# A SwiGLU behind attention: the last head pair's late loads in a new order, and PSUM banks as a ring of pairs

## The chip, the cores and the metric

The kernel runs on one core of a Trainium2 chip. The metric is device time in microseconds (us). A core has five engines that run their own instruction streams: TensorE (PE, matrix products into PSUM), VectorE (DVE), ScalarE (ACT), GpSimd (POOL) and SyncE (SP, which mostly issues DMAs; ACT issues some too). They wait for each other through semaphores.

## The reference, cut to what matters

```
def _attn_ref(q, k, v):                       # 4 x 8 x 576 x 64
    q_rot, k_rot = (rotate(q), rotate(k))
    scores = scale * np.matmul(q_rot, k_rot.transpose(0, 1, 3, 2))
    scores = scores - np.max(scores, axis=-1, keepdims=True)
    attn = np.exp(scores)
    attn = attn / (np.sum(attn, axis=-1, keepdims=True) + 1e-09)
    return np.matmul(attn, v).astype(np.float32)

def _moe_ref(x, w_gate, w_val, w_out):        # x: 2304 x 512, d_ff 1536
    g = x @ w_gate
    silu = g * (1.0 / (1.0 + np.exp(-g)))
    val = x @ w_val
    return (silu * val @ w_out).astype(np.float32)
```

x is the attention's result with the heads side by side: 4 batches of 576 rows make 2304 tokens. The inputs are float32, except that the weights enter the kernel as 64-bit words, of which DVE, ACT and POOL make a high and a low float32 part. Every product is made of three matmuls (high by high, high by low, low by high).

## The kernel before, in words

**Attention.** 32 heads make 16 pairs p of 9 blocks b of 128 rows; n counts the 144 blocks. For each block PE makes the scores (sc), DVE their row maxima (L364), ACT the exponential (L382), PE transposes it (tr, L425) and later multiplies by V (pv, L465). ACT copies the results (Y, L470), which go to device memory (yd: L484, L489, L490). Row sums go there as their reciprocals (rd, L403) and come back spread over partitions (R, rload, L630). During the last pairs, POOL already makes the tokens' high and low parts for the SwiGLU: `xload` (L637) brings Xab, `xprep` (L644 to L647) adds, multiplies by R and splits into xa, xm and xb. The late tokens (second half, tiles 1 and 2) are prepared after the attention by `xlate` on ACT and DVE (L666 to L681), from T0h and T2h, which `yload(t, i)` brings (L655, four DMAs each; i = 0 three quarters of the heads, i = 1 the rest).

**The plain stage.** Behind the attention come 12 units (`UNITS`): a weight tile f, a half s and a token tile t. Unit u multiplies first the gate's and then the value's weights, each 12 matmuls of 128x384 into a PSUM accumulation bank (`mm`, L793). Then `ev` takes the gate's bank through the Silu on ACT (L807), and multiplies by the value's bank on DVE (L808). A bank is free for the next unit when its reader is done. Banks come from `ch()`, which goes round the list `chp` with the counter `nch`; `open_chain` adds banks to it. f = 0's weights lie in FO, f = 1's in w0h/w0l (gate) and w1h/w1l (value). Units 0 and 1 are mixed with the last block's transposes and pv products. In the code the plain stage's function gives the order of units 1 to 11 and of the work between them.

**The second tile's weights.** `wfirst(1, i)` loads 512 KB (gate for i = 0, value for i = 1) and `bits9` takes it through six steps on DVE (L751 to L757), a cast on ACT (L738), and a subtraction and an addition on POOL (L739, L740). Before, both weights use one buffer, raw0, whose last third is scratch (X); the gate's steps stand in the attention's last pair, where the table `c1` has them (`conv1`), and the value's are run by `plain` (`first`). The next weights, for Strassen, come through `Stream` and `Conv`: loads L779, aux steps on DVE and ACT (L752 to L758), sums on POOL (L917 to L920) and the split into W (L695).

**Behind it** stand a Strassen product (`strassen`, ten products of L841) whose operands T0, T1, T2 are made in the plain stage (`forms` L701 on POOL, splits L695, the last of them from POOL's sums Z), and the down projection (`Down`, L1459).

**What sets the order.** From the last pair on PE, and in the plain stage also ACT, DVE and SP, run in the order in which the code is written; POOL does throughout. In the attention, SP's order from block 48 on is a scheduler's. A DMA of SP or ACT raises one of eight counters in turn, and its issue waits for the DMA that was issued eight earlier in the program's order on the same counter.

Of the kernel before, what the change touches and what calls it, by code (L numbers as in the profile page):

```python
# [10 lines left out]
FP32 = mybir.dt.float32  # L11
F32R = mybir.dt.float32r
U32 = mybir.dt.uint32
# [489 lines left out]
BK = 384  # L503
# [5 lines left out]
class Moe:  # L509
# [57 lines left out]
    def open_early(self, ctx, yctx):  # L567
        def pool(name, bufs):
            return yctx.enter_context(self.tc.tile_pool(name=name, bufs=bufs, reuse_waits="tile", side="right"))
        one = pool("m_y", 1)  # L570
        self.Ya = self.own(one, "T0h", [128, 2, 4, BK], FP32)
        self.Yb = self.own(one, "T2h", [128, 2, 4, BK], FP32)
        one = ctx.enter_context(self.tc.tile_pool(name="m_one", bufs=1, reuse_waits="tile", side="right"))
        self.Wb[1] = self.wbuf(one, 1)
        self.slot["raw0"] = ctx.enter_context(self.tc.tile_pool(name="m_raw0", bufs=1, reuse_waits="tile", side="right"))

    def open_late(self, ctx):
        def pool(name, bufs, **kw):
# [19 lines left out]
    def open_chain(self, ctx, n, **kw):  # L598
        p = ctx.enter_context(self.tc.tile_pool(name=f"m_c{len(self.chp)}", bufs=n, reuse_waits="tile",
                                                space=bass.MemoryType.PSUM, **kw))  # L600
        self.chp += [p] * n
        self.nch = 0

    def open_aux(self, ctx, n):
        self.aux_p = ctx.enter_context(self.tc.tile_pool(name=f"m_aux{n}", bufs=n, reuse_waits="tile",
# [159 lines left out]
    def wfirst(self, f, i):  # L765
        if f == 0:
            tmp = self.again(f"xa1{'hl'[i]}", [128, 1536], U32, "raw")
        else:
            tmp = self.again("raw0", [128, 1536], U32, "raw")
        self.nc.sync.dma_start(out=tmp[:, 0:1024], in_=self.wsrc(i, f))  # L770
        raw, X = tmp[:, 0:1024].rearrange("p (f t) -> p f t", t=2), tmp[:, 1024:1536]
        if f == 0:
            return self.bits10(raw, X, *self.Wb[f][i])
        go = lambda: self.bits9(raw, X, *self.Wb[f][i], self.nc.gpsimd)
        return go

    def rawload(self, src):
        raw = self.raw_p.tile([128, 1024], U32, name="raw")
# [151 lines left out]
def attn_swiglu(ctx: ExitStack, tc: tile.TileContext, qk, vr, wg, wv, wo, main, tail, out):  # L930
# [6 lines left out]
    NP = B * H // 2  # L937
    NB = NP * 9
    keep, pl, mctx = ExitStack(), ExitStack(), ExitStack()
    moe = Moe(tc, keep, pl, yd, rd, hd, od, wg, wv, wo, out)  # L940
# [97 lines left out]
    @step  # L1038
    def conv1(n, p, b):
        for i, at_ in enumerate(P["c1"]):  # L1040
            if p == NP - 1 and b == 7 * i:
                cv1[i] = moe.wfirst(1, i)()
            for _ in range(at_.count(b) if p == NP - 1 and i == 0 else 0):
                tc.keep_in_program_order(cv1[i].pop(0)())

    P, cvq, cv1 = PLAN, {}, {}
# [1 line left out]
    ctl0.__enter__()  # L1048
    ctl1 = tc.manual_schedule(engines={mybir.EngineType.PE})
    ctl1.__enter__()  # L1050
    ynext = [1, 2]
    for n in range(NB):
        p, b = divmod(n, 9)
        if n == 9:
# [21 lines left out]
    ctl2.__enter__()  # L1076
    scx.close()
    cctx, xctx = ExitStack(), ExitStack()
    moe.open_chain(cctx, 4)
    for _ in range(2):  # L1080
        moe.ch()
    ps = [moe.mm(0, 0, 0, 0)]
    at.trans(NB - 1)
    at.pv_some(10)
# [15 lines left out]
    moe.open_chain(cctx, 2, side="right")  # L1100
    moe.open_aux(xctx, 2)
    J, S, T0 = plain(moe, ps, cv1[1])
    ctl2.__exit__(None, None, None)
    ctl.__exit__(None, None, None)
# [15 lines left out]
def run(ops, n=99):  # L1120
    while ops and n:
        ops.pop(0)()
        n -= 1
# [37 lines left out]
def plain(moe, ps, first):  # L1161
    nc = moe.nc
    ve, po = nc.vector, nc.gpsimd
    J = [Conv(moe, 1 + s // 2, s % 2, s % 2) for s in range(10)]
    jobs = []

    def job(kind, x, h=0):
        if kind == "w":
            jobs.append((lambda: J[x].load(h), lambda: J[x].bits(h, ve)))
        else:  # L1170
            jobs.append((lambda: moe.oload(x, h), lambda: moe.obits(x, h)))

    o = [(h, fp) for fp in range(NFP) for h in range(2)]
    for s in range(10):
        job("w", s, 0)
        if s >= 4:
            job("o", *o.pop(0))
        job("w", s, 1)
        if s in (5, 8):
            job("o", *o.pop(0))  # L1180
    for x in o:
        job("o", *x)
    S = Stream(moe, jobs)
    ps = {1: ps}

    def mm(u):
        ps[u] = [moe.mm(*UNITS[u], i) for i in range(2)]

    def ev(u):
        moe.ev(u, ps.pop(u))  # L1190

    def T1(c):
        run(moe.split(ve, *(t[:, :, c] for t in moe.T[1]), moe.Z[c]))

    def st(n=1):
        run(moe.late, n)

    def T0(c):
        Tl[c] = moe.again(f"T0l{c}", [128, 4, BK], F32R, "T0l")
        run(moe.split(po, Th[:, :, c], Tl[c], Z[c]))  # L1200

    S.load()
    S.load()
    moe.rload(1, 1, None, 2)
    moe.rload(1, 1, None, 3)
    moe.yload(1, 1)
    moe.rload(1, 2, moe.R12)
    moe.yload(2, 1)
    F1 = [moe.forms(1, c, moe.Z[c], po) for c in range(2)]
    run(F1[0], 3)  # L1210
    run(first)
    run(F1[0])
    x1, x2 = moe.xlate(1), moe.xlate(2)
    mm(2)
    S.sign()
    run(S.take(1))
    ev(1)
    run(F1[1], 2)
    mm(3)
    run(S.take(1, False))  # L1220
    ev(2)
    st(2)
    run(J[0].sums(po))
    run(F1[1], 1)
    w = [J[0].split(x, po) for x in range(2)]
    run(x1, 3)
    mm(4)
    ev(3)
    run([w[0][0], w[1][0], w[0][1], w[1][1]])
    run(F1[1])  # L1230
    run(x1, 4)
    mm(5)
    ev(4)
    run(x1)
    run(x2, 3)
    st(2)
    mm(6)
    ev(5)
    run(x2, 3)
    mm(7)  # L1240
    ev(6)
    run(x2)
    mm(8)
    ev(7)
    T1(0)
    T1(1)
    Z = [moe.r_p.tile([128, 4, BK], FP32, name="R"), moe.again("T0l0", [128, 4, BK], FP32, "Z")]
    for c in range(2):
        run(moe.forms(0, c, Z[c], po))
    mm(9)  # L1250
    ev(8)
    T2 = moe.forms2(ve)
    run(T2, 2)
    mm(10)
    ev(9)
    st(9)
    run(T2)
    Th, Tl = moe.T[0] = [moe.again("T0h", [128, 4, 2, BK], F32R, "T0h"), [None, None]]
    mm(11)
    ev(10)  # L1260
    S.sign()
    dq = S.take(1)
    run(dq, 2)
    ev(11)
    st(9)
    run(dq)
    return J, S, T0
# [55 lines left out]
BANK = "XZWYXXY"  # L1323
# [8 lines left out]
class Down:  # L1332
# [90 lines left out]
    def run(self):  # L1423
        nc, m = self.nc, self.moe
        ve, ac = nc.vector, nc.scalar
        self.open()
        self.oload(4)
        self.oload(5)
        nc.sync.dma_start(out=m.hd[2][NFP - 1], in_=m.G[2])
        self.oload(6)  # L1430
        N = 3 * 7
        bank = {}
        for s in range(N):
            n, k = divmod(s, 7)
            more = n < 2
            for f in zip(self.sums(s + 2), self.form(s + 1)):
                run(list(f))
            if n == 0 and 1 < k < 5:
                self.osplit(k + 2)
            if s == 2:  # L1440
                nc.sync.dma_start(out=m.hd[0][NFP - 1], in_=m.G[0])
            if more and k == 3:
                w = self.where
                self.where = {"B11": w["TT"], "B22": w["B22"], "B21": w["B12"], "B12": w["B11"], "TT": w["B21"]}
            for b in {3: ("B11",), 4: ("B22",), 5: ("B21", "B12")}.get(k, ()) if more else ():
                self.load(n + 1, b)
            Oh, Ol = self.O[k]
            hi, lo = self.H[s % 2]
            for j in range(2):
                c = BANK[k], j  # L1450
                new = k == BANK.index(BANK[k])
                if new:
                    bank[c] = m.chp[0 if BANK[k] in "XW" else 5].tile([128, 512], FP32, name="ch")[:, 0:BK]
                ps = bank[c]
                d = slice(128 * j, 128 * j + 128)
                for f in range(NFP):
                    h = Oh[f // 3][:, f % 3, d]
                    for x, (l, r) in enumerate(((h, hi), (h, lo), (Ol[:, f, d], hi))):
                        nc.tensor.matmul(ps, l, r[:, f], start=(new and f == 0 and x == 0),  # L1459
                                         stop=(f == NFP - 1 and x == 2), skip_group_check=True)  # L1460
                t = {x: self.t[x][:, j] for x in self.t}
                if k in COPY:
                    ac.copy(t[COPY[k]], ps)
                for o in ADD.get(k, ()):
                    ve.tensor_tensor(out=t[o], in0=ps, in1=t[o], op=ALU.add)
                    self.out(n, o, j)
# [27 lines left out]
```

## Time and profile before

| what | us |
|---|---|
| time, median of 3 runs | 700.94 (699.97 to 701.76) |
| the profiled execution's own time | 700.15 |
| its span in the trace | 698.4 |
| PE busy | 680.0 (97%) |
| DVE busy | 576.3 (83%) |
| POOL busy | 468.6 (67%) |
| ACT busy | 424.8 (61%) |

The span runs from the first to the last instruction. PE's share of busy time is an average over stages; where PE is not busy is read from its waits and from its order of time. A busy PE can be a slow PE, so the granted clock is read beside it. An idle engine matters only where PE waits for what it makes, at once or later. The last block's work and the plain stage lie between about 276 and 337 us of the span, the Strassen product behind it.

### The profile page before, as it was taken

The numbers are of one execution on the slowest core, as the hardware profiler recorded it, in microseconds if no ns is written. First come the engines' busy times: TensorE is split into PE (matmuls) and PEld (weight loads), VectorE is DVE, ScalarE is ACT, GpSimd is POOL, SyncE is SP. The second block draws the span as 40 slices with busy tenths as digits, with TensorE's granted clock in tenths as the row PEclk, the third lists the DMA queues.
The fourth block names the chain that finished last, engine by engine and source line by source line (L and its number), as shares of the span: only waits on it lengthen the run. The fifth ranks groups of instructions, "written<-read, shape, count | busy, mean of one in ns | idle before, by whom it ended". The sixth has DMA issues, their size and how long they took to land.

```text
span 698.4 us, 12666 instructions
## 1 busy us (share of the span) xinstructions
PE 680.0 (97%) x4414; PEld 666.4 (95%) x4414; DVE 576.3 (83%) x883; ACT 424.8 (61%) x873; POOL 468.6 (67%) x475
## 2 busy tenths in 40 slices
PE   8999999999999999899999999999999999999998
PEld 6899999999999998899999999999999999999997
DVE  5888898888888889389978787989988599877683
ACT  5899998888888887246553433424534375444341
POOL 8899799999999976598879589398794630000000
PEclk9999999999999999999999999999999999999999
DMA  6897899779987989771214427255355897517101
GB/s 190 191 242 204 218 227 251 198 205 251 236 213 198 236 216 235 184 214 45 76 61 149 152 96 245 99 188 181 112 206 189 252 335 249 204 51 249 62 23 68
DMA packets 78784, 125.76 MB, mean 180 GB/s; under 512 B 16880, under 2 KB 55680, under 8 KB 78720
## 3 DMA queue, kind: packets, MB, share of 16 engines
q1 hardware_dynamic: 75248, 118.77, 60.1%
q10 hardware_dynamic: 3472, 6.18, 2.4%
q8 instruction: 35, 0.57, 0.3%
q14 instruction: 29, 0.24, 0.1%
HBM read 66.91 MB, written 33.10 MB: 143 GB/s over the span
## 4 chain that ended last, share of the span: by engine, by line
PE 73%; DVE 11%; DMA 6%; ACT 4%; issue 3%; SPq 1%; POOL 0%; DVEq 0%; ACTq 0%; POOLq 0%
PE ch L841 25%; PE ch L1459 15%; PE pv L465 11%; PE sc L349 11%; PE tr L425 8%; PE tr L289 2%; DVE dB L1397 2%; ACT E L382 1%; DMA raw<-in_moe_w_val_dram 1%; DMA rd<-rr 1%; ACT N L308 1%; DVE dO L1378 1%; DMA yd<-Y 1%; PE pv L229 1%; DVE aux L753 1%
## 5 line engine op out<-in xcount | busy, mean ns | idle before, releaser
L364 DVE TENSOR_REDUCE nmt<-sc 128x1 f32<-128x576 f32 x144 | 108.2, 751 | 20.3 <-PE sc L349 18.9
L382 ACT ACTIVATE E<-sc,nmt 128x576 f32<-128x576 f32 x128 | 97.3, 760 | 2.3 <-DVE nmt L364 2.2
L425 PE MATMUL tr<-ident,E 128*128 128x128 f32 x512 | 77.0, 273 | 0.4 <-DVE ET1l L427 0.2
L425 PEld LDWEIGHTS tr<-ident,E 128*128 128x128 f32 x512 | 61.1, 140 | 3.4 <-PE tr L289 1.4
L1459 PE MATMUL ch<-dW,dO 128*128 128x384 f32 x216 | 63.8, 336 | 0.4 <-DVE dW L1407 0.4
L206 POOL TENSOR_TENSOR t<-X,tab 128x256 f32<-128x256 f32 (+2 forms) x94 | 54.1, 597 | 9.9 <-DMA X<-in_qk_dram 6.2
L349 PE MATMUL sc<-QK 128*128 128x288 f32 x240 | 58.7, 326 | 1.3 <-ACT E L382 0.4
L426 ACT CAST ET2h<-tr 128x512 fp32r<-128x512 f32 x80 | 47.1, 589 | 15.6 <-PE tr L425 15.4
L427 DVE TENSOR_TENSOR ET2l<-tr,ET2h 128x512 fp32r<-128x512 f32 x80 | 53.1, 682 | 2.7 <-ACT ET2h L426 2.6
L349 PE MATMUL sc<-N,QZ 128*128 128x288 f32 x240 | 51.5, 296 | 0.0
L695 POOL TENSOR_TENSOR W<-WF,W 128x1024 fp32r<-128x1024 f32 x20 | 48.0, 2414 | 3.6 <-ACT W L695 3.6
L208 POOL TENSOR_TENSOR rot<-rot,t 128x512 f32<-128x512 f32 (+2 forms) x47 | 47.0, 1000 | 3.7
L427 DVE TENSOR_TENSOR ET1l<-tr,ET1h 128x512 fp32r<-128x512 f32 x64 | 43.0, 685 | 7.0 <-ACT ET1h L426 6.7
L207 POOL TENSOR_TENSOR rot<-X,tab 128x512 f32<-128x512 f32 (+2 forms) x47 | 46.9, 999 | 0.0
L841 PE MATMUL ch<-T0h,W 128*128 128x384 f32 x160 | 44.3, 338 | 1.6 <-DVE R L816 1.6
L1459 PE MATMUL ch<-dH,dO 128*128 128x384 f32 x156 | 45.4, 337 | 0.0
L426 ACT CAST ET1h<-tr 128x512 fp32r<-128x512 f32 x64 | 36.8, 596 | 13.1 <-PE tr L425 13.1
L841 PE MATMUL ch<-T2h,W 128*128 128x384 f32 x160 | 44.4, 338 | 0.0
L841 PE MATMUL ch<-T1h,W 128*128 128x384 f32 x160 | 43.9, 335 | 0.0
L465 PE MATMUL pv<-ET2h,VS 128*128 128x320 f32 x128 | 40.8, 329 | 1.1 <-ACT ET2h L426 0.9
L845 ACT COPY uz<-ch 128x384 f32<-128x384 f32 x30 | 14.4, 479 | 44.5 <-PE ch L841 40.1
L349 PEld LDWEIGHTS sc<-QK 128*128 128x128 f32 x240 | 36.9, 190 | 4.0 <-ACT E L382 4.0
(349 smaller groups left out, 2325.5 us busy)
## 6 DMA issues: line engine op xcount, KB each, us to landing
QK<-N SPq DMA_DIRECT2D x64, 288.0 KB, 4.4
hd<-sg SPq DMA_DIRECT2D x14, 768.0 KB, 4.0
dB<-hd SPq DMA_DIRECT2D x8, 1152.0 KB, 6.9
X<-in_qk_dram SPq DMA_DIRECT2D x15, 576.0 KB, 5.2
yd<-Y SPq DMA_DIRECT2D x31, 256.0 KB, 4.4
raw<-in_moe_w_gate_dram SPq DMA_DIRECT2D x12, 512.0 KB, 4.9
raw<-in_moe_w_val_dram SPq DMA_DIRECT2D x12, 512.0 KB, 3.8
Xab<-yd SPq DMA_DIRECT2D x32, 192.0 KB, 5.0
```

The source lines that it names most:

```text
L206: e.tensor_tensor(out=sel(t2, u), in0=sel(x, w), in1=tb(Sn, u), op=ALU.mult)
L208: e.tensor_tensor(out=o, in0=o, in1=t2, op=ALU.add)
L349: nc.tensor.matmul(ps[:, g, 0:288], l, rr[:, o + g * 288:o + (g + 1) * 288], start=(x == 0), stop=(x == len(terms) - 1))
L364: nc.vector.tensor_reduce(out=nmcol, in_=ps[:, :, 0:288], axis=AX.XY, op=ALU.max, negate=True)
L382: nc.scalar.activation(out=E.rearrange("p (a b) -> p a b", a=2), in_=ps[:, :, 0:288], func=ACTF.Exp, bias=nmcol, scale=1.0, accum_out=self ...
L425: nc.tensor.transpose(ps[:, c], E[:, o + c * 128:o + (c + 1) * 128], self.ident)
L426: nc.scalar.copy(dst[0], src)
L427: nc.vector.tensor_tensor(out=dst[1], in0=src, in1=r32(dst[0]), op=ALU.subtract)
L465: nc.tensor.matmul(st["ps"][:, 0:w], VS[:, sl, :], t, start=(x == 0), stop=(x == last))
L695: return [lambda: self.nc.scalar.copy(h, f), lambda: le.tensor_tensor(out=l, in0=f, in1=r32(h), op=ALU.subtract)]
L841: nc.tensor.matmul(acc, l[:, w, c * 128:(c + 1) * 128], r, start=(n == 0 and k not in ONTO), stop=(n == 5), skip_group_check=True)
L1459: nc.tensor.matmul(ps, l, r[:, f], start=(new and f == 0 and x == 0), stop=(f == NFP - 1 and x == 2), skip_group_check=True)
```

## The change

The code's diff has three parts. First, the value weight of the second tile gets a buffer of its own, raw1, of 1024 columns; the scratch stays in raw0's last third. `wfirst(1, 1)` is called in block 1 of the last pair in place of block 7, one block behind the gate's. Its steps still run in `plain`. Second, of the late tokens' early loads only `yload(1, 0)` stays in the last pair; `yload(2, 0)` goes to `plain`, between `yload(1, 1)` and the load of R12. Third, the banks: before, a pool of four was opened, two banks of it were passed over, and two more were opened behind unit 1, with the counter set to 0 each time. Now three pools of two are opened, the first two in reversed order, and the counter goes on, behind unit 1, with the new pair; every unit takes the next pair of a ring of three. `Down` takes its banks by the counter.

```
@@ open_early
-        self.slot["raw0"] = ctx.enter_context(self.tc.tile_pool(name="m_raw0", bufs=1, reuse_waits="tile", side="right"))
+        self.slot["raw0"] = self.slot["raw1"] = ctx.enter_context(self.tc.tile_pool(name="m_raw0", bufs=1, reuse_waits="tile", side="right"))
@@ open_chain
         self.chp += [p] * n
-        self.nch = 0
+        self.nch = len(self.chp) - n
@@ wfirst
-            tmp = self.again("raw0", [128, 1536], U32, "raw")
+            tmp = self.again(f"raw{i}", [128, (1536, 1024)[i]], U32, "raw")
+        if (f, i) != (1, 1):
+            self.X1 = tmp[:, 1024:1536]
         self.nc.sync.dma_start(out=tmp[:, 0:1024], in_=self.wsrc(i, f))
-        raw, X = tmp[:, 0:1024].rearrange("p (f t) -> p f t", t=2), tmp[:, 1024:1536]
+        raw, X = tmp[:, 0:1024].rearrange("p (f t) -> p f t", t=2), self.X1
         if f == 0:
             return self.bits10(raw, X, *self.Wb[f][i])
-        go = lambda: self.bits9(raw, X, *self.Wb[f][i], self.nc.gpsimd)
-        return go
+        return self.bits9(raw, X, *self.Wb[f][i], self.nc.gpsimd)
@@ conv1
-            if p == NP - 1 and b == 7 * i:
-                cv1[i] = moe.wfirst(1, i)()
+            if p == NP - 1 and b == i:
+                cv1[i] = moe.wfirst(1, i)
@@ attn_swiglu
-    ynext = [1, 2]
+    ynext = [1]
...
-    moe.open_chain(cctx, 4)
-    for _ in range(2):
-        moe.ch()
+    moe.open_chain(cctx, 2)
+    moe.open_chain(cctx, 2)
+    moe.chp.reverse()
+    moe.nch = 0
     ps = [moe.mm(0, 0, 0, 0)]
@@ plain
     moe.yload(1, 1)
+    moe.yload(2, 0)
     moe.rload(1, 2, moe.R12)
@@ Down
-                    bank[c] = m.chp[0 if BANK[k] in "XW" else 5].tile([128, 512], FP32, name="ch")[:, 0:BK]
+                    bank[c] = m.chp[(m.nch + "X.Z.W".index(BANK[k].replace("Y", "Z"))) % 6].tile([128, 512], FP32, name="ch")[:, 0:BK]
```

In the changed file the same lines stand one further down from L772 on (`mm` L794, the Silu L808, the multiply L809), and three further down at the end.

On SP, in the last pair, the gate load has left its place behind the QK loads (L319 to L323); both second-tile weights now stand right ahead of two Strassen weight loads (before L779, now L780). Rows with a minus are of before, rows with a plus of after.

```order
 L637 DMA Xab<-yd_57 64x2x384 x2
-L779 DMA raw<-in_moe_w_gate_dram 128x1024 x2
+L772 DMA raw<-in_moe_w_gate_dram 128x1024
+L772 DMA raw<-in_moe_w_val_dram 128x1024
+L780 DMA raw<-in_moe_w_gate_dram 128x1024 x2
 L637 DMA Xab<-yd_57 64x2x384
 L484 DMA yd_57<-Y_3992 128x2x256
 L637 DMA Xab<-yd_57 64x2x384
-L655 DMA T0h<-yd_57 64x3x384
 L637 DMA Xab<-yd_58 64x2x384 x2
-L655 DMA T2h<-yd_57 64x3x384
 L655 DMA T0h<-yd_57 64x3x384
```

Two weight loads stand where none did, ahead of the last Xab loads, and the last two Xab loads (of yd_58) stand ahead of all four DMAs of `yload(1, 0)`. The gate load that stood 24 rows higher is gone there.

Further down on SP, at the end of the last pair:

```order
-L655 DMA T0h<-yd_57 64x3x384
-L655 DMA T2h<-yd_57 64x3x384
-L484 DMA yd_58<-Y_4239 128x2x256
-L770 DMA raw<-in_moe_w_val_dram 128x1024
+L484 DMA yd_58<-Y_4241 128x2x256
 L630 DMA R<-rd 64x4x128 x2
 L630 DMA R<-rd 64x4x256 x2
```

`yload(2, 0)` (its last two DMAs are the first rows) and the value load have left their places ahead of the R loads; the four DMAs of `yload(2, 0)` now stand behind `yload(1, 1)`.

On PE only the waits change around units 2 and 3 (ch is the bank with its number, xa1 and xm1 the tokens, FO the first tile's weights; "Activation" and "Pool" are waits for ACT and POOL). Before, the end of unit 2 and the start of unit 3:

```order
L793 MATMUL ch_4543<-xa1h_3562,FO_84 128x384 x2
L793 MATMUL ch_4543<-xa1l_3563,FO_84 128x384
L793 MATMUL ch_4543<-xa1h_3562,FO_84 128x384
L793 MATMUL ch_4572<-xm1_75,FO_84 128x384 [waits Activation_49,Pool_49]
L793 MATMUL ch_4572<-xm1_75,FO_84 128x384 [waits Pool_49]
```

and now:

```order
L794 MATMUL ch_4544<-xa1h_3562,FO_84 128x384 x2
L794 MATMUL ch_4544<-xa1l_3563,FO_84 128x384
L794 MATMUL ch_4544<-xa1h_3562,FO_84 128x384
L794 MATMUL ch_4573<-xm1_75,FO_84 128x384 [waits Pool_49] x2
L794 MATMUL ch_4573<-xm1_75,FO_84 128x384
```

The wait of unit 3's first matmul for ACT, the Silu of unit 1, is gone. Unit 0's first matmul has likewise lost a wait for ACT, the exponential of the last block. Unit 4's first matmul, which before waited for nothing but PE, now waits for unit 1's Silu. In one place PE's rows move: the first three matmuls of the Strassen product stand ahead of unit 11's last twelve. DVE's, ACT's and POOL's rows keep their order. On ACT the store L490 waits, before and after, for the DMA eight issues earlier on its counter: before and now this is an R load of 64x4x128 elements.

## Rows read from the trace of the kernel before

**Rows 1.** Waits of PE from 260 to 480: us in total, times, longest

```profile
PE ch L793 <- POOL raw L739: 3.3, 1, 3.3
PE ch L841 <- DVE R L816: 1.6, 1, 1.6
PE ch L793 <- ACT Et L382: 1.5, 1, 1.5
PE ch L841 <- ACT uz L851: 1.3, 1, 1.3
```

**Rows 2.** Stretches of 5 us: us and count per engine, granted clock, DMA share, GB/s

```profile
265.00:270.00 5.00, 5.00 (x40) 4.87 (x39) 4.10 (x8) 3.72 (x10) 4.61 (x6) 1.00 0.93 283
...
295.00:300.00 5.00, 1.83 (x6) 1.86 (x7) 4.69 (x8) 2.54 (x5) 3.32 (x3) 0.83 0.86 209
```

**Rows 3.** PE in order of time: start, us, operation [idle before <- releaser]

```profile
278.29 2.38 PE L793 MATMUL ch<-xa,FO 128*128 128x384 f32 x12 [1.55 <-ACT Et L382]
...
298.17 2.11 PE L793 MATMUL ch<-xm,FO 128*128 128x384 f32 x6 [3.29 <-POOL raw L739]
...
301.90 1.20 PE L793 MATMUL ch<-xm,FO 128*128 128x384 f32 x6
...
303.98 0.51 PE L793 MATMUL ch<-xa,w0h 128*128 128x384 f32 x2
...
343.94 0.44 PE L841 MATMUL ch<-xb1h,W 128*128 128x384 f32 x1 [1.29 <-ACT uz L851]
```

**Rows 4.** ACT in order of time, 288 to 316

```profile
288.68 0.43 ACT L470 COPY Y<-pv 128x320 f32<-128x320 f32 x1 [3.07 <-PE pv L465]
...
294.19 0.40 ACTq L490 DMA_DIRECT2D yd<-Y  x1
295.86 0.67 ACT L738 CAST w1h<-raw 128x512 fp32r<-128x512 f32 x1 [6.76 <-DVE raw L755]
...
297.54 0.86 ACT L807 ACTIVATE Xab<-ch 128x384 f32<-128x384 f32 x2
...
315.44 0.50 ACT L666 COPY aux<-T0h 128x384 f32<-128x384 f32 x1
```

**Rows 5.** DVE in order of time, 269 to 302

```profile
269.21 0.42 DVE L751 TENSOR_SCALAR raw<-raw 128x512 uint32<-128x512 uint32 x1
...
283.95 0.56 DVE L808 TENSOR_TENSOR Xab<-ch,Xab 128x384 f32<-128x384 f32 x1 [1.03 <-ACT Xab L807]
293.75 0.43 DVE L751 TENSOR_SCALAR raw<-raw 128x512 uint32<-128x512 uint32 x1 [9.24 <-DMA raw<-in_moe_w_val_dram]
...
297.10 0.70 DVE L753 TENSOR_SCALAR aux<-aux 128x512 f32<-128x512 f32 x1
...
301.41 0.55 DVE L808 TENSOR_TENSOR Xab<-ch,Xab 128x384 f32<-128x384 f32 x1
```

**Rows 6.** POOL in order of time, 281 to 333

```profile
281.73 1.02 POOL L645 TENSOR_TENSOR Xab<-Xab,R 128x384 f32<-128x384 f32 x1
...
288.43 1.86 POOL L701 TENSOR_TENSOR T0l<-xa1h,xa1l 128x768 f32<-128x768 f32 x1 [3.98 <-PE pv L465]
...
296.61 1.56 POOL L739 TENSOR_TENSOR raw<-raw,w1h 128x512 f32<-128x512 f32 x1 [4.38 <-ACT w1h L738]
...
329.00 3.30 POOL L701 TENSOR_TENSOR Z<-xa 128x768 f32<-128x768 f32 x1 [2.12 <-DVE T1l L695]
```

**Rows 7.** DMA issues from 236 to 310: operation, count, KB each, us to landing

```profile
R<-rd SPq DMA_DIRECT2D x2, 256.0 KB, 4.4
...
R<-rd SPq DMA_DIRECT2D x2, 128.0 KB, 8.4
```

**Rows 8.** SP in order of time, at 260

```profile
260.65 1.09 SPq L779 DMA_DIRECT2D raw<-in_moe_w_gate_dram  x2
```

**Rows 9.** DMA issues of those two loads, one by one, as in rows 7

```profile
raw<-in_moe_w_gate_dram SPq DMA_DIRECT2D x1, 512.0 KB, 7.4
...
raw<-in_moe_w_gate_dram SPq DMA_DIRECT2D x1, 512.0 KB, 8.1
```

## The prediction

> **What bounds the kernel now.** I read the waits of TensorE (PE) in the stretch around the change first [rows 1]: the reader is to see that after 260 us PE waits only four times for longer than 1 us, 7.7 us in all, and that two of the four lie in the stage that is changed. The table of 5 us stretches then shows what the longest wait does besides [rows 2]: PE is busy 1.83 of 5 us from 295 on, and the granted clock falls to 0.83, between the two levels 1.2 and 2.4 GHz. PE's order of time [rows 3] puts the waits in their places: 1.55 us ahead of unit 0 (278.29), 3.29 us ahead of unit 3 (298.17), 1.29 us in the first Strassen product (343.94). From there on PE waits once more, 1.6 us [rows 1]; so what PE is early at 344 us the end is early too, and whatever does not reach 344 us is worth nothing.
>
> The profile puts the 3.29 us down to a POOL subtraction (L739). But the order gives unit 3's first matmul a wait for ACT, the Silu that frees unit 1's bank, and that Silu (the first of two from 297.54, 0.86 us together) ends just ahead of 298.17 [rows 4]. It is late because ACT, in its order, has the cast of w1h in front of it, which waited 6.76 us, to 295.86, for VectorE's (DVE's) L755; DVE in turn had waited 9.24 us for the value weight's load [rows 4, 5]. So one late load stands behind three engines: DVE starts on w1 at 293.75, POOL at 296.61, and DVE on the next weight (aux) at 297.10 [rows 5, 6]. These two chains reach PE again at 343.94: PE waits there for a copy on ACT, which stands behind a cast of POOL's Z sums, and Z started at 329.00 after waiting 2.12 us for DVE's split of T1 [rows 6].
>
> **The change part by part.** The sum is made against the profiled execution (700.15 us: a span of 698.4 and 1.75 around it) and its gain is then taken off the median, 700.94, which is 0.8 above it.
>
> *The ring of banks.* Unit 0's first bank held, before, the scores of the last block, so PE waited for their exponential; it now holds those of an earlier block and waits for PE's own scores. The transposes ahead of it had ended, and its operands (xa, FO) are older: 1.55 us go [rows 3]. Unit 2 takes the two new banks; unit 3 takes unit 0's, whose multiply ended at 283.95 + 0.56 [rows 5]: 3.29 us go. The gap's aftermath goes with it: unit 3's first half of 12 matmuls ran from 298.17 to 301.90, 3.73 us, the second at full clock from 301.90 to 303.98, 2.08 us [rows 3]; 1.65 us go. PE's own sum is 1.55 + 3.29 + 1.65 = 6.49 us: it begins unit 4 at 297.5 in place of 303.98. What is late next on PE: unit 4 now waits for unit 1's Silu and multiply, which follow the w1 chain. Before, the Silu began 1.68 us behind the w1h cast (297.54 against 295.86 [rows 4]), and the multiply at 301.41 [rows 5]; below, the chain is 5.76 us earlier, which puts the multiply's end at 301.41 + 0.55 - 5.76 = 296.2, ahead of 297.5. The three Strassen matmuls that now stand ahead of unit 11's last twelve are the same work, 0; and the Down stage's two added waits are for sums made one 6 us product earlier, 0.
>
> *The early value load.* DVE no longer waits at 293.75; it can begin once the multiply of unit 0 is done, at 283.95 + 0.56 - 1.55 = 283.0, and be through w1's six steps (from 293.75 to 297.10 at most before, 3.35 us) at 286.4 [rows 5]. That does not start the chain then, because ACT's cast of w1h stands behind two stores. The first (L489) waits for the second pv copy, 288.68 + 0.43 [rows 4], now 1.55 earlier: 287.56, and takes 0.40. The second (L490, 294.19 before) is issued when the DMA eight issues earlier on the round of eight completion counters has landed. Before and after that is an R load. It waits for POOL's multiply L645 to end, 281.73 + 1.02 = 282.75 [rows 6], and before it also stood behind yload(2,0) and the value load; now it is issued right behind that, at about 283.3. Its landing bounds the chain from both sides: 8.4 us, as the same loads took before among the value load and four others, and 4.4 us, as the next R loads took, twice the size [rows 7]. The queue in front of it is emptier now, but POOL or the DMAs ahead may be later (below), so I take the middle, 6.4: L490 at 289.7. With its 0.40 the cast begins at 290.1, and the aux step 1.24 behind (297.10 - 295.86), at 291.34: 297.10 - 291.34 = 5.76 us earlier. On POOL three sums of T0l stand in front (from 288.43, waiting for PE's pv, one of 1.86 us and two of half its size: until 292.15, now 290.6), and L739 begins 0.75 behind the cast, at 290.85: 296.61 - 290.85 = 5.76 too [rows 4, 6]. The ends: with 4.4, L490 is held by L489 at 288.0, DVE's chain is 7.46 earlier and POOL's 6.0; with 8.4, L490 is at 291.7 and both are 3.76 earlier.
>
> *What moves on SP.* The gate load goes back past 24 other issues to just ahead of the two gate loads at 260.65 [rows 8], the value load follows it at once: four 512 KB loads where two stood. The third and fourth are Strassen's and are not urgent. Two things are. The gate's own landing: DVE reads it at 269.21, with the row maxima of the attention behind it [rows 5]; the two loads from 260.65 on took 7.4 and 8.1 us [rows 9], so the first in line lands at 268.1 to 269.1 (the later end if it waits for PE as the second of the two now does): 0 to 0.3 us late, taken at 0. And the Xab loads behind the four: the stretch moves 283 GB/s at a DMA share of 0.93 [rows 2], so 1.05 MB more is 3.7 us more at most; they feed POOL's L645 and so the R load. The cost is between 0 and 3.7 us of the chain; part of it is inside the middle taken above. Against it, the two Xab loads of the last chunk no longer stand behind a yload, a gain of about as much as an issue or two.
>
> One page of the Trainium skill bears on the four loads, DMA: Bandwidth & Descriptors, section Queues, rings and completion order: on each engine descriptors are consumed in the order of the ring, though completions need not come in the order of issue. The rows agree so far as they go: the two loads landed in order, about 1.2 us apart [rows 9]. By that rule the gate, being first, lands as before and the cost is 0; were the four to share evenly it would land with the last, some 3 us late, and the sum would be 2.8 us in place of 5.76.
>
> *yload(2,0) later.* Four loads of 288 KB leave the stretch ahead of the R load, and stand behind the four small yload(1,1). At 0.6 us of issue each they push SP's R12 loads by 2.4 us. They are issued by about 297 and first read by ACT's copy that began at 315.44 [rows 4], now 309.7. The cover is over 12 us, so the cost is 0; if it were gone, up to 2.4.
>
> *The sum.* PE is 6.49 us early, the chain 5.76; PE's wait at 343.94 grows from 1.29 to 2.0 us, and 5.76 reaches the end: 700.94 - 5.76 = **695.2 us**. On the profiled execution that is 700.15 - 5.76 = 694.4. As for the bounds: PE cannot bring more than 6.49 + 1.29 = 7.78, and the late landing leaves 3.76.
>
> **The rivals.**
> *The chain is as early as PE.* The R load lands in 4.4 us and POOL's slack (the 2.12 us ahead of Z) takes up what POOL lacks: 6.5 to 7.8 us, 693.1 to 694.4. For it: fewer DMAs in front; against it: something always comes next.
> *Half of it.* Either the Xab loads are 3.7 late and the R load lands at 293.4 (297.10 - 295.04 = 2.1 us, 698.8), or the wait at 343.94 grows enough to lower the clock, as 3.29 us did and 1.29 to 1.55 us did not: 5.76 - 1.65 = 4.1, and with the slow landing 2.1. In all 697.2 to 698.8.
> *The change does not do what it says.* The value is early, but the cast stays where it was because the store in front of it lands no sooner, as its 8.4 us row allows if its issue is not earlier either: PE's 6.49 us turn into a wait of 7 us at 344. Gain 0 to 1.5: 699.4 to 701.
> *Slower.* The gate load is 24 issues later than before. If the four loads and the Xab loads choke each other and the first takes twice what the second of two took, 16.2 us, it lands at 277.2; DVE reads it 8.0 us late, and the maxima, exponentials and PE's scores behind it with it: 8.0 - 5.76 = 2.2 us slower, 703.2. It decides from a landing 5.76 us after 269.21, at 275.0. Against it: 7.4 and 8.1 us is what such loads took in this very place, at a DMA share of 0.93 [rows 2, 9].
>
> **How the numbers follow.** Forecast (3.8 to 6.5 us gained, 694.4 to 697.2) 0.54; as early as PE 0.10; half of it 0.16; nothing 0.12; slower 0.08. A measurement of this kernel can tell 0.3%, 2.1 us, from no change: the first three are faster by more, 0.80; same 0.12; slower 0.08. The range reaches from the cap of 7.8 us, 693.1, to 699.9: that leaves out the slower case and most of the case of nothing.
>
> **What would show it.** Right: no wait of PE ahead of unit 0 and unit 3, and a granted clock of 1.00 from 295 to 300; DVE's first w1 step near 283; ACT's L490 between 288 and 291.7, the w1h cast right behind it, POOL's subtraction near 291; PE's wait in the first Strassen product between 1 and 3 us. Wrong: a wait of PE for maxima or exponentials from 270 to 278 (the gate late), a wait over 3 us ahead of 344 with a lower clock, or the cast still near 295.

## The result, and the profile after

The changed kernel takes 693.69 us in the median of five runs (693.12 to 696.08), the kernel before 700.26 beside it. The ratio of the two is 0.9912, with a 95% interval from 0.9888 to 0.9936: 0.6 to 1.1% faster. The forecast was 5.76 us of gain; 6.2 us is what the ratio gives (0.0088 of 700.3), and the profiled execution's span went from 698.4 to 691.5 us, 6.9 less. In absolute time the median lies 0.7 us under the 694.4 to 697.2 us that the prediction held most likely, and so in the range of its rival that has the chain as early as PE (693.1 to 694.4). But the kernel before was itself 0.7 us faster here than the 700.94 that the forecast started from; as a gain, 6.2 us lies inside the forecast's 3.8 to 6.5, near its end.

PE's waits from 255 to 480 us, the two over 1 us, answer to [rows 1]; behind them three stretches of 5 us as in [rows 2]:

```profile
PE ch L842 <- ACT uz L852: 1.9, 1, 1.9
PE ch L842 <- DVE R L817: 1.5, 1, 1.5
```

```profile
295.00:300.00 5.00, 5.00 (x31) 5.00 (x30) 4.83 (x9) 0.71 (x2) 4.84 (x5) 1.00 1.05 208
...
335.00:340.00 5.00, 3.14 (x18) 2.82 (x17) 5.00 (x10) 3.62 (x4) 3.42 (x2) 1.00 0.11 39
340.00:345.00 5.00, 5.00 (x31) 5.00 (x30) 3.30 (x6) 2.67 (x4) 5.00 (x3) 1.00 0.62 201
```

The two waits in the plain stage are gone, and from 295 to 300 PE is busy throughout at a granted clock of 1.00, where it had been 1.83 us and 0.83. The wait in the first Strassen product is left, and longer than before. In PE's order of time (as [rows 3]) units 0 and 3 begin without a wait, unit 4 at 297.29 in place of 303.98, and PE restarts in the Strassen product at 337.85 in place of 343.94:

```profile
276.75 2.34 PE L794 MATMUL ch<-xa,FO 128*128 128x384 f32 x12
...
293.13 1.20 PE L794 MATMUL ch<-xm,FO 128*128 128x384 f32 x6
...
297.29 0.51 PE L794 MATMUL ch<-xa,w0h 128*128 128x384 f32 x2
...
337.85 0.44 PE L842 MATMUL ch<-xb1h,W 128*128 128x384 f32 x1 [1.86 <-ACT uz L852]
```

So PE was 6.69 us early at unit 4 and 6.09 us early at the restart. The chain that it waits for is read on ACT, DVE and POOL (as [rows 4 to 6]):

```profile
287.55 0.45 ACTq L489 DMA_DIRECT2D yd<-Y  x1
288.04 0.48 ACTq L490 DMA_DIRECT2D yd<-Y  x1
288.61 0.67 ACT L738 CAST w1h<-raw 128x512 fp32r<-128x512 f32 x1 [1.09 <-DMA R<-rd]
...
303.67 1.05 ACT L695 CAST W<-WF 128x1024 fp32r<-128x1024 f32 x1 [0.49 <-POOL WF L921]
```

```profile
269.02 0.62 DVE L751 TENSOR_SCALAR raw<-raw 128x512 uint32<-128x512 uint32 x1
...
282.84 0.75 DVE L751 TENSOR_SCALAR raw<-raw 128x512 uint32<-128x512 uint32 x1
...
286.86 2.12 DVE L756 TENSOR_SCALAR raw<-raw 128x512 uint32<-128x512 uint32 x1
289.01 1.39 DVE L757 SCALAR_TENSOR_TENSOR raw<-raw 128x512 f32<-128x512 uint32 x1
290.33 0.69 DVE L753 TENSOR_SCALAR aux<-aux 128x512 f32<-128x512 f32 x1
291.05 0.70 DVE L754 TENSOR_SCALAR aux<-aux 128x512 uint32<-128x512 uint32 x1
```

```profile
275.37 1.02 POOL L644 TENSOR_TENSOR Xab<-Xab 128x384 f32<-128x384 f32 x1 [4.26 <-DMA Xab<-yd]
...
283.39 1.07 POOL L645 TENSOR_TENSOR Xab<-Xab,R 128x384 f32<-128x384 f32 x1
...
286.84 1.85 POOL L701 TENSOR_TENSOR T0l<-xa1h,xa1l 128x768 f32<-128x768 f32 x1 [0.57 <-DVE raw L755]
...
291.24 1.31 POOL L739 TENSOR_TENSOR raw<-raw,w1h 128x512 f32<-128x512 f32 x1
...
300.70 0.73 POOL L918 TENSOR_TENSOR WF<-WF 128x256 f32<-128x256 f32 x1
...
322.90 3.29 POOL L701 TENSOR_TENSOR Z<-xa 128x768 f32<-128x768 f32 x1 [1.70 <-DVE T1l L695]
```

The reader is to see the store L490 at 288.04 (before 294.19) with the cast right behind, DVE's first step on w1 at 282.84 (before 293.75), the next weight's at 290.33 (297.10), POOL's L739 at 291.24 (296.61) and Z at 322.90 (329.00). Z is 6.10 us early, and so is PE's restart. Between L739 and Z the chain runs through POOL's weight sums. Before, their first stood at 306.33:

```profile
306.33 0.74 POOL L917 TENSOR_TENSOR WF<-WF 128x256 f32<-128x256 f32 x1
```

They are 5.63 us earlier now, and ACT's cast behind them, which had not waited for them before, waits 0.49 us for the last. In run 6 below they come 2.6 us later than here, and Z comes 2.6 us later; in run 9 they come 1.4 us sooner, and Z only 0.4. So in the changed kernel POOL's part of the chain is the one that ends last, and little is gained by having it earlier still. The remaining 0.8 of the span's 6.9 us lie behind 344 us, most of it in the Down stage, where PE's waits for DVE's dW and dWF fell from 0.9 us to 0.3.

### The profile page after: what moved, and what is told of

Read it like the earlier page. It is cut to its first block, busy times and chain, and to the rows that moved or that the text cites. A ratio compares the mean times of both kernels' runs of the same rounds, so it can differ in the third digit from the quotient of the medians.

```text
span 691.5 us, 12667 instructions
## 1 busy us (share of the span) xinstructions
PE 677.5 (98%) x4414; PEld 664.5 (96%) x4414; DVE 579.8 (84%) x883; ACT 425.2 (61%) x873; POOL 470.1 (68%) x475
## 4 chain that ended last, share of the span: by engine, by line
PE 79%; DVE 9%; ACT 4%; DMA 4%; issue 2%; POOL 1%; SPq 0%; DVEq 0%; ACTq 0%; POOLq 0%
PE ch L842 23%; PE ch L1462 14%; PE pv L465 12%; PE sc L349 11%; PE tr L425 8%; PE ch L794 7%; PE tr L289 2%; ACT E L382 2%; DVE dB L1400 1%; DMA dO<-od 1%; DMA raw<-in_moe_w_val_dram 1%; DVE dW L1410 1%; ACT N L308 1%; DVE dO L1381 1%; PE pv L229 1%
## 6 DMA issues: line engine op xcount, KB each, us to landing
QK<-N SPq DMA_DIRECT2D x64, 288.0 KB, 4.2
```

## The experiments

Three parts of the change were taken apart (runs 1 to 4), then the terms of the sum that had come out otherwise (5 to 7, 9, 10), then the wait that is left and the clock behind it (8, 11). Each was timed beside the kernel before.

| run | median us | ratio to before, 95% interval |
|---|---|---|
| 1 ring alone | 701.37 | 1.0011 [0.9997, 1.0025] |
| 2 value load alone | 694.61 | 0.9919 [0.9907, 0.9931] |
| 3 value load and late yload(2,0) | 694.03 | 0.9911 [0.9898, 0.9924] |
| 4 ring and value load | 696.37 | 0.9941 [0.9928, 0.9954] |
| the changed kernel, once more | 693.99 | 0.9917 [0.9893, 0.9941] |
| 5 changed, two pools | 693.01 | 0.9900 [0.9883, 0.9917] |
| 6 changed, POOL's sums behind | 696.79 | 0.9949 [0.9931, 0.9967] |
| 7 changed, T0 cast behind | 694.17 | 0.9918 [0.9900, 0.9935] |
| 8 ring alone, T0 cast behind | 699.94 | 1.0002 [0.9991, 1.0012] |
| 9 two pools, weight sums forward | 693.32 | 0.9910 [0.9892, 0.9928] |
| 10 as 9, old banks | 694.54 | 0.9925 [0.9907, 0.9943] |
| 11 ring and value load, T0 cast behind | 695.89 | 0.9939 [0.9922, 0.9956] |

**1. The ring alone.** The kernel before with the third part of the diff:

```
-        self.nch = 0
+        self.nch = len(self.chp) - n
...
-    moe.open_chain(cctx, 4)
-    for _ in range(2):
-        moe.ch()
+    moe.open_chain(cctx, 2)
+    moe.open_chain(cctx, 2)
+    moe.chp.reverse()
+    moe.nch = 0
...
```

> Kernel before with the ring of bank pairs alone. Two chains (my theory): PE loses its 1.55 and 3.29 us waits and the slow clock, 6.5 us, but the value load lands where it did (DVE's first w1 step near 293.7), so PE runs into new waits ahead of units 4 and 5 and in the first Strassen product, there 5 to 8 us in all: 0 to 0.6 us faster than before, and if a wait over 3 us lowers the clock, up to 1.7 slower. Rival, PE's own waits are the whole gain: 6 to 6.5 us faster.

It is no faster. PE's waits from 255 to 480, and the stretch behind the last of them:

```profile
PE ch L841 <- ACT uz L851: 2.9, 1, 2.9
PE ch L793 <- DVE Xab L808: 1.9, 2, 1.6
PE ch L841 <- DVE R L816: 1.3, 1, 1.3
PE ch L793 <- ACT sv L807: 1.2, 1, 1.2
```

```profile
345.00:350.00 5.00, 4.77 (x18) 4.77 (x19) 4.33 (x9) 1.94 (x3) 5.00 (x3) 0.66 0.31 104
```

The waits ahead of units 0 and 3 (4.8 us together) are gone, and 3.0 us of new waits stand in units 4 and later and 1.6 us more at the Strassen product, with the low clock that unit 3 had had. PE's waits alone were not the gain. (This profile runs 1.7 us late already near 274 us. The ring does not explain that, as run 8, with the same ring, is not late there.)

**2 and 3. Without the ring.** Run 2 is the value load alone (first part of the diff), run 3 adds the second part.

```
-            if p == NP - 1 and b == 7 * i:
+            if p == NP - 1 and b == i:
...
```

> Kernel before with the early value load alone (old banks, yload(2,0) early). Two chains: the wait ahead of unit 3 goes because unit 1's Silu is early, the 1.55 us ahead of unit 0 stay, and the cast of w1h begins 1.5 us later than in the changed kernel, near 290: 4.2 to 5 us faster than before. Rival, the ring is what frees unit 3: under 1.5 us faster.

> The changed kernel with the old banks (value load early, yload(2,0) late). Two chains: 1.5 us slower than the changed kernel, 4.6 to 5.2 faster than before, 0 to 0.5 better than with the value load alone. Rival, the ring carries most: within 1.5 us of before.

Both beat what was expected: run 2 by 0.7 us at least, and run 3 has the changed kernel's time with the old banks. The wait ahead of unit 3 is gone here too, since unit 1's Silu is early; the 1.4 us ahead of unit 0 stay. That only half of these reach the chain is seen on DVE and POOL in run 3:

```profile
287.12 0.43 DVE L756 TENSOR_SCALAR raw<-raw 128x512 uint32<-128x512 uint32 x1
287.58 0.70 DVE L757 SCALAR_TENSOR_TENSOR raw<-raw 128x512 f32<-128x512 uint32 x1
291.05 0.70 DVE L753 TENSOR_SCALAR aux<-aux 128x512 f32<-128x512 f32 x1 [2.77 <-ACT aux L752]
```

```profile
288.08 1.90 POOL L701 TENSOR_TENSOR T0l<-xa1h,xa1l 128x768 f32<-128x768 f32 x1 [2.47 <-PE pv L465]
```

PE's pv products end 1.2 us later than with the ring, and POOL's sum starts later. DVE's L756 is done by then and L757 began 0.5 us ahead of it: 0.43 and 0.70 us, against 2.12 and 1.39 beside the sums in the changed kernel. The aux step is at 291.05, only 0.72 later than there. Z (323.60) and PE's restart (338.54) are 0.7 later too, while the span differs by 0.1 us; where the rest is made up behind the restart was not followed.

**4. Ring and value load, yload(2,0) early.**

```
-    ynext = [1]
+    ynext = [1, 2]
...
-    moe.yload(2, 0)
```

> The changed kernel with yload(2,0) in its early place. If the four loads lengthen the landing of the R load as they stand just ahead of it, the store L490 moves from 288.0 to 290 to 293 and the gain falls from 6.5 to 3 to 5 us. If the R load is held by POOL's multiply anyway and lands as fast, the gain stays within 0.7 us of the changed kernel's.

The gain is smaller than the changed kernel's by 2.4 to 2.7 us in the medians, by 1.7 to 2.0 in the ratios. The R load's landing (DMA issues from 284 on, KB each, us to landing; the changed kernel, then run 2, then run 4):

```profile
R<-rd SPq DMA_DIRECT2D x1, 128.0 KB, 3.5
```

```profile
R<-rd SPq DMA_DIRECT2D x1, 128.0 KB, 5.8
```

```profile
R<-rd SPq DMA_DIRECT2D x1, 128.0 KB, 6.5
```

With the four loads just ahead of it, it takes 5.8 to 6.5 us in place of 3.5, as the first reading had it, and L490 stands at 290.65. That carries the chain 1.4 us later (Z at 324.27 against 322.90). But run 2 has the same Z (324.25), the same restart of PE (339.18), and is 1.8 us faster than run 4. Both restarts, run 2 and run 4, and the stretch behind it in run 4:

```profile
339.18 0.44 PE L842 MATMUL ch<-xb1h,W 128*128 128x384 f32 x1 [1.75 <-ACT uz L852]
```

```profile
339.18 0.69 PE L842 MATMUL ch<-xb1h,W 128*128 128x384 f32 x1 [2.90 <-ACT uz L852]
```

```profile
340.00:345.00 5.00, 5.00 (x24) 5.00 (x24) 3.75 (x7) 1.85 (x3) 5.00 (x3) 0.77 0.33 105
```

The ring brings PE there 1.2 us sooner, it waits 2.90 us, and the clock is at 0.77 in the stretch behind. PE is busy throughout that stretch, so the clock takes some 1.2 us of work there (0.23 of 5 us, an estimate from this row). Here the ring costs time.

**5. Two pools.** By a pool for each weight buffer the gate load does not wait for the space that the value's needs, and goes back to its early place.

```
-        self.slot["raw0"] = self.slot["raw1"] = ctx.enter_context(self.tc.tile_pool(name="m_raw0", bufs=1, reuse_waits="tile", side="right"))
+        for i in range(2):
+            self.slot[f"raw{i}"] = ctx.enter_context(self.tc.tile_pool(name=f"m_raw{i}", bufs=1, reuse_waits="tile", side="right"))
```

> The changed kernel with the two weight buffers in pools of their own, by which the gate load goes back to its early place and three 512 KB loads stand where four did. Theory: POOL's wait for Xab falls from 4.3 us to about 1.5 to 3, its multiply L645 ends 1 to 1.7 us earlier, but the store L490 is held at 288.0 by L489 and the pv products, so the time stays within 0.7 us of the changed kernel's. Rival, the late Xab loads hold the chain: 1 us or more faster than the changed kernel.

POOL's wait for Xab falls to 2.09 us (with the same two pools it is 3.60 in run 9, so not all of the fall is shown to be theirs), and the time is 0.7 us under the changed kernel's first median, 1.0 under its second. The intervals overlap, so that it is faster is not shown, only that it is no slower. Its median is the lowest of the versions run. POOL, then DVE (lines stand one further down):

```profile
273.55 1.01 POOL L645 TENSOR_TENSOR Xab<-Xab 128x384 f32<-128x384 f32 x1 [2.09 <-DMA Xab<-yd]
...
287.50 1.86 POOL L702 TENSOR_TENSOR T0l<-xa1h,xa1l 128x768 f32<-128x768 f32 x1 [2.21 <-DVE raw L758]
```

```profile
286.80 0.69 DVE L758 SCALAR_TENSOR_TENSOR raw<-raw 128x512 f32<-128x512 uint32 x1
```

This time DVE's six steps are through when POOL's sum begins, and the last two take 0.43 (L757) and 0.69 us. That the sum begins just as DVE's step ends, at 287.49, is chance, although the row names DVE as what released it: in every profile with the sum in this place it begins 0.09 to 0.10 us behind the start of the last pv product, and so it does here (287.41).

**6. POOL's three sums behind the w1 steps.**

```
-    run(F1[0], 3)
     run(first)
     run(F1[0])
```

> The changed kernel with POOL's first three sums of T0l behind the w1 steps in place of ahead of them. Theory: DVE's L756 and L757 then take 0.43 and 0.7 us in place of 2.12 and 1.39, as no POOL sum runs beside them, and POOL's L739 begins near 289.3 in place of 291.24; but POOL stands idle for 3 us first, so its chain behind (weight sums at 300.7) is 1.5 to 2 us later, and the wait ahead of the fourth Strassen product grows: 1 to 2 us slower than the changed kernel, more if the wait passes 2.9 us and lowers the clock. Rival, DVE's w1 steps set the end: 0.5 to 1.5 us faster.

The theory held, by the branch with the lower clock: 3.1 us slower than the changed kernel. L756 and L757 take 0.43 and 0.69 us, POOL's L739 begins at 290.00 (289.3 expected); the weight sums come at 303.31, 2.6 us later than in the changed kernel (1.5 to 2 expected), ACT waits longer for them, Z starts at 325.51, and PE waits 2.9 us and finds a clock of 0.50 (ACT, then PE's longest wait, then the stretch behind it):

```profile
306.28 1.06 ACT L695 CAST W<-WF 128x1024 fp32r<-128x1024 f32 x1 [2.44 <-POOL WF L921]
```

```profile
PE ch L842 <- ACT uz L852: 2.9, 1, 2.9
```

```profile
340.00:345.00 5.00, 4.59 (x14) 4.59 (x15) 3.48 (x7) 2.12 (x3) 4.95 (x3) 0.50 0.31 102
```

**7 and 8. The cast of T0h behind the copy that PE waits for.** PE's restart waits for ACT's copy of uz, which stands in ACT's order behind a cast of Z.

```
-    at(0, 0, 0, lambda: T0(1))
+    at(0, 0, 2, lambda: T0(1))
```

> The changed kernel with the cast of T0h from Z placed on ACT behind the copy (L852) for which PE waits, in place of ahead of it. Theory: PE's 1.86 us at 337.85 are a wait for ACT's order alone; the copy then follows the product at once and the wait falls to 0.5 to 0.8: 1.0 to 1.4 us faster than the changed kernel. Rival, the products that need T0 come too soon behind: the wait moves there, within 0.5 us.

> The ring of banks alone, with that cast behind the copy. Theory: the ring's gain was there and was lost in the wait of 2.87 us and the lower clock behind it; with the wait at 0.5 to 0.8 us and the clock full, 3 to 4 us faster than the ring alone, about 3 faster than before. Rival, units 4 and 5 had used it up already: under 1.5 us faster than the ring alone.

Both theories fell, and both rivals held. Run 7 is no faster than the changed kernel, run 8 0.6 us faster than the ring alone (by ratios 0.0009, within their intervals). PE's waits in run 7 from 255 on:

```profile
PE ch L842 <- DVE R L817: 1.5, 2, 1.3
PE ch L842 <- DVE sg L817: 0.7, 1, 0.7
PE ch L1462 <- DVE dW L1410: 0.6, 2, 0.4
PE ch L842 <- ACT uz L846: 0.3, 1, 0.3
```

The wait for uz at L852 is gone and comes back in pieces, nearly all of them for DVE (in run 8 one of 1.7 us for DVE's sg). The scheduler also set POOL's later rows anew in these two, so the edit is not quite alone. What stands behind PE there is then DVE's stream, so ACT's order was not all of it.

**9 and 10. The weight sums forward, and the ring again.** On the two pools, one sum of T0l is moved behind POOL's weight sums; run 10 has the old banks besides.

```
-    run(F1[1], 2)
+    run(F1[1], 1)
     mm(3)
...
     run(J[0].sums(po))
-    run(F1[1], 1)
+    run(F1[1], 2)
```

> Two pools, and POOL's weight sums (L918 to L921 of the changed kernel) moved one T0l sum of 1.0 us further forward. Theory: DVE's chain waits 2.07 to 2.19 us near 305 for ACT, and ACT for those sums; 0.5 to 0.95 us of that wait go and the chain to the Strassen product with them: 0.5 to 1 us faster than two pools alone (693.0). Rival, DVE's order from there on takes it back: no difference from two pools.

> The same kernel with the old banks. Theory, the end follows the chain of w1, DVE and POOL, and PE's 1.4 us ahead of unit 0 cost only what they delay the last pv products by: 0.3 to 1 us slower than with the ring. Rival, PE's waits count in full: 1.4 us slower; or not at all, as between the changed kernel and the one without the ring: within 0.3 us.

DVE's wait near 305 ends 1.1 us sooner than in run 5 (run 5's stood at 305.14), but Z only 0.4 (322.52), and the time is no better: the rival.

```profile
304.03 0.57 DVE L668 TENSOR_TENSOR aux<-aux,T2h 128x384 f32<-128x384 f32 x1 [1.60 <-ACT aux L667]
```

Run 10 against run 9 is 1.2 us for the ring, where run 3 and the changed kernel gave 0 to 0.3. Given the early value and the late yload, the ring is thus worth between nothing and 1.2 us; the intervals of all four overlap, and the runs don't settle it closer.

**11. Run 4 with the cast behind the copy**, the edit of run 7.

> Ring and early value load with yload(2,0) early, and the cast of T0h behind the copy for which PE waits. Theory: this kernel without the cast's move started Z on POOL at the same time as the one without the ring (324.3) and still was 1.8 us slower, because PE's wait of 2.9 us lowered the granted clock to 0.77; with a wait below 2 us the clock stays at 1.00 and it is 1.5 to 2.5 us faster than without the move (696.4). Rival, the 1.8 us were lost elsewhere: within 0.5 us of 696.4.

In its profile the clock stays at 1.00 and the span is 1.5 us shorter than run 4's (693.6 against 695.1), but the median only 0.5 us. The size that was expected is not there; the wait went to DVE, 1.7 us for its sg. All six executions of run 11 have a mean granted clock of 1.000, all six of run 4 one of 0.997 to 0.999. So either the moved cast loses most of what the clock gives back (in run 7 it gained nothing either), or the clock was the lesser part of run 4's 1.8 us over run 2. The runs don't separate the two.

**The changed kernel once more**, unedited, beside runs 9 to 11.

> The changed kernel once more, beside the three below. 693 to 694.5 us; its wait ahead of the fourth Strassen product near 1.9 us.

Its profile shows something else than the first. The two stretches around PE's wait, which was 1.8 us:

```profile
335.00:340.00 5.00, 3.22 (x17) 2.90 (x16) 5.00 (x10) 3.61 (x4) 3.34 (x2) 0.92 0.11 39
340.00:345.00 5.00, 5.00 (x24) 5.00 (x23) 3.03 (x6) 1.55 (x2) 5.00 (x3) 0.74 0.46 144
```

The same wait, 1.86 us in the first execution and 1.8 here, left the clock at 1.00 once and lowered it to 0.74 once; the spans were 691.5 and 692.8.

The mean clock of every execution is on record, and it bears on what the ring is worth. Of the 15 executions of the changed kernel eight have 1.000 and take 692.4 to 694.1 us (median 693.2). Four have 0.998, as the profile above, and take 694.0 to 696.1. Three have 0.999 (694.2, 695.1 and 701.2); such a value can also come from the last microseconds, where PE has nothing left to do, as in run 3's profile. Run 3 itself has a median of 694.03. In the two-pool kernel the three executions at 1.000 take 693.1 to 693.3 us with the ring (run 9), and the six without it, all at 1.000, 693.7 to 695.5 (run 10). So while the clock stays full the ring looks worth 0.8 to 1.4 us, and where its longer wait at the restart lowers the clock it gives that back. This is sorted from the executions afterwards; no run was made to test it.

One table sums up, from the profiles of the kernels with the cast in its old place, the start of Z on POOL, PE's wait at its restart, the lowest clock of the two stretches from there, and the span:

| kernel | Z, us | wait | clock | span | span less Z |
|---|---|---|---|---|---|
| before | 329.00 | 1.29 | 1.00 | 698.4 | 369.4 |
| run 1 | 330.33 | 2.87 | 0.66 | 700.8 | 370.5 |
| run 2 | 324.25 | 1.75 | 1.00 | 692.8 | 368.6 |
| run 3 | 323.60 | 1.34 | 1.00 | 691.6 | 368.0 |
| run 4 | 324.27 | 2.90 | 0.77 | 695.1 | 370.8 |
| changed | 322.90 | 1.86 | 1.00 | 691.5 | 368.6 |
| changed, again | 323.10 | 1.8 | 0.74 | 692.8 | 369.7 |
| run 5 | 322.90 | 1.2 | 1.00 | 690.9 | 368.0 |
| run 6 | 325.51 | 2.9 | 0.50 | 697.0 | 371.5 |
| run 9 | 322.52 | 1.8 | 1.00 | 691.5 | 369.0 |
| run 10 | 323.68 | 1.2 | 1.00 | 692.6 | 368.9 |

With the clock at 1.00 the end comes 368.0 to 369.4 us behind Z, with a lower clock 369.7 to 371.5. PE's own progress does not show in the last column, but as a longer wait.

## Why the prediction was right, point by point

- **The end follows the lesser of two gains, the w1 chain's.** Right: chain 5.76 forecast, 6.10 measured at Z; PE 6.49 forecast, 6.69 measured at unit 4; the wait at the restart 2.0 forecast, 1.86 measured. Runs 1, 2 and 3 show it directly: PE's part without the chain is worth nothing, the chain without the ring nearly everything. That the chain came within 0.4 us is in part luck, as two errors of the sum offset each other: the landing was put too late and the work of DVE and POOL behind it too short (below).
- **The ring takes away 1.55, 3.29 and 1.65 us.** The sizes are right, the part they were given to is not: with the ring alone they go and come back; with the value load alone (run 2) the 3.29 us and the clock behind them go too, since the Silu that unit 3 waited for is early. The ring's own part is the 1.55 us ahead of unit 0.
- **The R load's landing sets L490.** Right as a mechanism; as a size the middle of 6.4 us was too long. POOL's L645 ended 1.7 us later than forecast (283.39 + 1.07 = 284.46, behind an Xab wait of 4.26 us), and the load was issued at 284.49 in place of 283.3; but it landed in 3.5 us, under the lower bound of 4.4, at 288.0. L489 ended at 288.0 too, so what L490 waited for was met by both at once, and the profile can't tell which came last; in runs 2 and 4 the landing did (289.95 and 290.65). The short landing was the premise of the rival that has the chain as early as PE; the next two terms kept it from coming true in full.
- **w1's six steps on DVE take 3.35 us, done at 286.4.** Wrong: they took 7.5 us, to 290.3, and so DVE, not ACT, was the last to be ready for the aux step. This term was taken from a stretch [rows 5] in which POOL stood idle, waiting 4.38 us for ACT [rows 6]; the steps were moved beside POOL's work. It cost the chain 0.4 to 0.5 us: the cast at 288.61 and 1.24 behind it would have given 289.85. The too long landing hid it in the sum.
- **POOL's three sums take 3.7 us.** They took 1.85, 1.21 and 1.46, and L739 began 0.39 late against the forecast 290.85. Same cause. POOL's part was the one that ended last: 5.63 us early at the weight sums, and the rest of Z's 6.10 is about half a us that ACT's cast behind them had in hand before.
- **The gate load is in time.** Right: it was issued at 260.74, took 7.3 us and landed at 268.0, DVE read it at 269.02. The value load behind it took 7.8. The first in line landed first, at 268.0 against 269.3. The Trainium skill, page DMA: Bandwidth & Descriptors, section Queues, rings and completion order, has each DMA engine take its descriptors in the order of the ring, without promising that completions keep that order; these landings agree with it. The even share that the prediction set against it, by its own estimate some 3 us more, is not seen. The slower rival never came near.
- **yload(2,0) late costs 0.** Right, and it gains: about 2 us beside the ring (the changed kernel against run 4), 0.6 without it (run 3 against 2, whose times overlap). The prediction had it as an emptier queue and gave it no price of its own.
- **A longer wait could lower the clock.** The rival was there in waiting: at 1.86 us the first execution escaped it, at 1.8 the second did not. The forecast had no term for it; that the profiled execution had the full clock is luck.

## What to carry to other kernels

A wait that the profile charges to the busiest engine is worth what the next meeting point of the chains lets through: follow both chains to the place where they meet again, and take the lesser gain. Where a step is moved, price it beside its new neighbours, not by its row in the old place; here that was wrong by a factor of two. And a bank order that lets TensorE run ahead of a chain it will wait for can lose time, when the one long wait that it makes lowers the clock, as in run 4 beside run 2.

## What the runs showed of the hardware

- **Some DVE steps and POOL's sums hold each other up.** A DVE step of 0.43 us (L756) took 2.12 when a POOL sum had begun 0.02 us ahead of it: the sum ended at 286.84 + 1.85 = 288.69, the step at 288.98. The sums behind it, 1.02 us before the change, took 1.21 and 1.46. Away from the sums (run 6), or begun ahead of them (run 3), the steps take 0.43 and 0.69 to 0.70. No wait row shows it on DVE's side, only the long operation. The Trainium skill, page SBUF — State Buffer, section SBUF: two separate sides, has this as an exclusive lock on a port pair that the two share, held for a whole instruction by whichever starts first; of DVE's operations it counts in only those in a two-port mode or with two SBUF inputs. The traces agree for w1's steps. Not every DVE step is held up: those of the next weight, with their scratch (aux) in PSUM, take 0.69 to 0.70 us from 291 on although POOL is busy beside them.
- **The clock after a wait of TensorE.** In the profiles waits of 1.2 to 1.75 us left it at 1.00, those near 2.9 lowered the mean of a stretch of 5 us to 0.50 to 0.77 each of three times, and waits near 1.8 us did so in one of three. The length alone does not decide: a wait of 2.15 us in run 8 (298.67, behind ACT's Silu) left it at 1.00.
- **A store on one queue waits for a load on another.** ACT's L490 has nothing to do with the R load on SP but shares its completion counter; it moved from 294.19 to 288.04 as that load's landing did (285.79 + 8.4 before, 284.49 + 3.5 now).
